# Batch 2's keys handled in the second stage, a new instruction order, paired numerators and one block-diagonal key product

## The chip, the cores and the metric

The kernel runs on one core of one Trainium2 chip. The metric is the device time of one launch in microseconds (us), on that core. Three runs of the kernel before took 995.9, 994.68 and 989.43 us; the median is 994.68 us.

## The reference

Random-feature attention, whose result is fed through a two-layer network. Cut to what matters:

```python
batch, n_heads, seq, head_dim = (8, 8, 576, 64);  n_features = 128
def phi(x):                                  # x is scaled by 64**-0.25
    h = einsum('bhsd,md->bhsm', x, omega) - sum(x * x, -1) / 2
    return exp(h - max(h, -1)) / sqrt(m)
q_p, k_p = phi(q_s), phi(k_s)
kv  = einsum('bhsm,bhsd->bhmd', k_p, v)      # one 128 x 64 matrix per batch and head
z   = sum(k_p, axis=2)
num = einsum('bhsm,bhmd->bhsd', q_p, kv)
den = einsum('bhsm,bhm->bhs', q_p, z)[..., None] + 1e-06
x   = (num / den), heads side by side        # 4608 tokens x 512
h = x @ w_in                                 # 512 -> 2048
out = (h - tanh(h)) @ w_out                  # 2048 -> 512
```

All inputs and the output are float32, and the network's weights are read as float32 too.

## The kernel before, in words

**Pairs of heads.** The eight heads are taken two at a time, so there are four pairs `c` for each batch `b`, and one unit of key work is one (batch, pair): 576 tokens of two heads, whose 64 dimensions each fill the 128 partitions.

**Chunks of tokens.** The 4608 tokens are cut into chunks by `SIZE`. For a chunk `ch` the query units (`q_unit(ch, c)`, one for each pair) give the attention result of that chunk, and the network then runs over 16 slices of 128 hidden features: 12 matmuls (L540) give `h`, ScalarE takes the tanh, VectorE subtracts, ScalarE and VectorE split the result in a high and a low part, and three matmuls for each 128 tokens (L563 to L565) add to the output. These network matmuls are of the type fp32r, with each operand split in a high and a low part, so that a product is made of three.

**Two kinds of attention work.** In the first stage, keys and queries are *native*: `native_k` and `native_q` multiply plain float32. TensorE runs each of their products as two instructions, so the trace counts two matmuls for one in the code. For one pair, `native_k` projects 4 tiles of 128 tokens for each head (L921: two products at a time, one on the upper 64 rows of the array and one on the lower), then the last 64 tokens of both heads (L923, each product 64 rows and 64 columns), takes the least of each row (L927, L936) and the exponentials (L932, L940), multiplies with the values (L944, L954), and turns the sums `z` by two transposes (L971). In the second stage, `k_unit` and `q_unit` split the operands into high and low parts and use fp32r: 9 key projections of 256 columns (L453), a rounded copy of the exponentials (`key_hi`, L715), its rest (`key_lo`, L719), the same for the values (L723, L727), and 10 products of 256 columns (L736). The sums `z` and the results are turned through DRAM there, by 12 DMAs of SyncE for each unit instead of the two of a native unit. The numerators of a query unit (L663) are plain float32 products on half the array's columns each, and VectorE multiplies them by the reciprocals (L682).

**Which batch is where.** `K2 = 4` makes the keys of batches 0, 1 and 2 native (12 units); batches 3 to 7 (20 units) are `k_unit`s. Six native query units cover the first three chunks of 256 tokens.

**The weights.** They come as 16 blocks of 1 MB in a packed form, loaded by ScalarE's queue (`d*.is`) and unpacked by ScalarE, GpSimd and VectorE (`decoder`, L1087 to L1132), while the first stage runs. A block's first network slice needs it unpacked. The network of the first 512 tokens is `feed` (`f0` to `fd`, and `f0e`, `f0f`).

**What sets the order.** The order is written out by hand, as two long strings of tokens. `ORDER` is the first stage, `LATER` the second. A token names a unit, one of its steps and places in PSUM or SBUF: `k02.pk0.2` is the first value product of batch 0, pair 2, in PSUM bank 2; `q40.m.0` is the numerators of chunk 4, pair 0. Each engine executes its own instructions strictly in this order, so an instruction that waits holds up everything behind it on its engine. `EARLY` names two loads that go to ScalarE's queue; all other loads go to SyncE's.

Of the kernel before, what the change touches and what calls it, by code (L numbers as in the profile page):

```python
# [44 lines left out]
k00.pj.2.3.4 k12.lv.2 q11.expB.1 q01.lq.0 k02.pj.5.6.7 k00.redB k00.red5 k00.expB.2 k00.redA k13.lk.0 k02.redA  # L45
k00.expA.3 k03.pj.0.1.3 k23.lk.1 k02.red5 k02.redB k03.vc k02.exp5.0 k02.expA.4 d1.is k12.vc k03.redB k02.pk0.2
k02.expB.5 k03.red5 k03.redA q01.pj.7.5 k03.exp5.1 k03.expA.6 k02.pk1 q01.redB k03.expB.7 q01.redA k13.pj.6.3.0
k02.z k13.lv.0 k02.kvf q01.expA.4 k03.pk0.1 k01.lk.2 k00.exp5.0 k13.redB q01.expB.5 k13.redA k02.zt k03.pk1
k11.lk.0 k13.expB.6 k13.red5 k23.pj.7.4.5 k02.zb k00.lv.1 k03.z k13.expA.7 q11.den0 k13.exp5.1 k03.zt d0.is
d1.b.0 k13.vc q11.nD0 k13.pk0.3 q11.nA0 k23.red5 k23.redB k03.kvf k03.zb k23.redA q11.pt0.2 d1.cl k23.expB.7  # L50
k13.pk1 q11.den1 q11.qt0.0 k11.pj.6.0.1 k13.kvf q11.nD1 k23.expA.6 q11.nA1 k13.z q01.den1 k01.lv.0 k00.vc
k23.exp5.1 q11.pt1.4 k13.kvwa k00.pk0.2 k11.red5 q11.qt1.1 k10.lk.1 q01.nA1 k11.redB q11.pn.7 k11.redA
d0.b.1 k20.lk.0 q01.nD1 k13.zt q01.den0 k00.pk1 q11.xh q10.lq.0 d0.cl k13.zb k11.expA.0 q11.xl q01.pt1.5
k23.lv.1 k00.z q01.nA0 d0.v1 k11.exp5.0 k00.zt q01.qt1.0 k01.pj.4.3.7 k01.vc k00.kvf d0.v2 k00.zb d4.is
k11.expB.1 k10.pj.6.1.5 k01.redA k01.red5 k01.expA.3 k01.redB q10.pj.2.0 k10.redA k01.expB.2 k10.redB k01.pk0.4
q01.nD0 k12.lk.2 k23.vc k10.red5 d0.v3 k23.pk0.3 k10.expA.3 k21.lk.1 k23.pk1 k10.expB.6 q10.redB q10.redA
q00.lq.0 q01.pt0.6 k01.exp5.1 k23.z d0.hi d1.v1 k01.pk1 k10.lv.1 d1.v2 d0.nh k23.zt k01.kvf k11.lv.0 d1.v3
# [1178 lines left out]
```

## Time and profile before

| | |
|---|---|
| median of 3 runs | 994.68 us (989.43 to 995.9) |
| the profiled execution | 992.21 us, its span 990.4 us |
| TensorE matmuls (PE) busy | 976.7 us, 99% |
| weight loads (PEld) | 810.1 us, 82% |
| VectorE (DVE) | 749.2 us, 76% |
| ScalarE (ACT) | 592.1 us, 60% |
| GpSimd (POOL) | 48.9 us, 5% |
| first network slice starts | 66 us |
| second chunk's network starts | 164.5 us |
| last matmul starts | 986.03 us |

The span is the part of the time that the profiler sees, so the profiled execution has 1.8 us around it. A row of the timeline gives the start of a group of equal instructions and how long it lasted to the end of its last one. Matmuls overlap, so the time that one takes from TensorE is read from the start of one row to the start of the next, not from the length of a row. A table by stage gives, for each stretch, how long each engine was busy in it and how many instructions it started.

### The profile page before, as it was taken

The page shows a single profiled execution, that of the slowest core. Times are in us where ns is not written, and L with a number is a line of the kernel's source. Part 1 is how long each engine was busy: PE and PEld are TensorE (multiplying, and loading weights), DVE is VectorE, ACT ScalarE, POOL GpSimd, SP SyncE. Part 2 cuts the span into 40 slices and gives each one's busy share as a digit, 9 for nine tenths or more (in the row PEclk, how much of TensorE's full clock was granted, in tenths as well). Part 3 has the DMA queues.
Part 4 walks back from the last instruction along what each step waited for, and adds up shares of the span by engine and source line. Part 5 has one row for each costly group of instructions (what it writes and reads, how often), then busy time and mean ns, then how long its engine had stood idle before and what let it go on. Part 6 is the DMA issues. An engine that isn't in the chain of part 4 may idle for free.

```text
span 990.4 us, 16846 instructions
## 1 busy us (share of the span) xinstructions
PE 976.7 (99%) x5260; PEld 810.1 (82%) x5260; DVE 749.2 (76%) x2772; ACT 592.1 (60%) x1497; POOL 48.9 (5%) x83
## 2 busy tenths in 40 slices
PE   9999999999999999999999999999999999999998
PEld 8787778887888888888878888788877787888886
DVE  5988887998998999989999998998577533223222
ACT  8996767685766786667656776675455332123222
...
GB/s 261 246 241 187 236 189 129 162 130 148 125 94 144 115 85 159 136 117 109 116 169 124 137 120 144 137 87 128 68 99 123 118 49 38 1 1 43 0 1 43
DMA packets 96601, 117.84 MB, mean 119 GB/s; under 512 B 19456, under 2 KB 62848, under 8 KB 96512
## 3 DMA queue, kind: packets, MB, share of 16 engines
...
q8 instruction: 42, 0.69, 0.3%
q14 instruction: 47, 0.39, 0.1%
...
## 4 chain that ended last, share of the span: by engine, by line
PE 84%; DVE 7%; ACT 3%; DMA 3%; issue 1%; SPq 1%; POOL 0%; ACTq 0%; DVEq 0%; POOLq 0%
PE h L540 35%; PE po L563 11%; PE po L565 11%; PE po L564 11%; PE pn L663 3%; PE pj_q L592 3%; PE pk L736 2%; PE k_pk L944 1%; DMA xs<-over 1%; PE pj_k_B L453 1%; PE pj_k_A L453 1%; DMA raw<-w 1%; PE k_pj L921 1%; DVE zf L1015 1%; DVE a L1118 1%
## 5 line engine op out<-in xcount | busy, mean ns | idle before, releaser
L540 PE MATMUL h<-xa,w 128*128 128x512 f32 (+2 forms) x1920 | 420.4, 368 | 1.7 <-DVE zf L551 1.7
L540 PEld LDWEIGHTS h<-xa,w 128*128 128x128 f32 x1920 | 340.5, 188 | 54.5 <-DVE zf L551 1.9
L563 PE MATMUL po<-w,zr 128*128 128x512 f32 x544 | 213.8, 393 | 0.6 <-ACT zr L553 0.6
L565 PE MATMUL po<-w,zr 128*128 128x512 f32 x544 | 212.7, 391 | 0.6 <-DVE zr L555 0.6
L564 PE MATMUL po<-w,zr 128*128 128x512 f32 x544 | 212.7, 391 | 0.0
L845 DVE TENSOR_TENSOR zf<-h,zf 128x512 f32<-128x512 f32 (+1 forms) x138 | 90.5, 656 | 147.4 <-ACT zf L844 146.0
L844 ACT ACTIVATE zf<-h 128x512 f32<-128x512 f32 (+1 forms) x138 | 78.7, 570 | 202.1 <-PE h L540 199.7
L565 PEld LDWEIGHTS po<-w,zr 128*128 128x128 f32 x544 | 102.1, 188 | 23.9 <-DVE zr L555 1.9
L563 PEld LDWEIGHTS po<-w,zr 128*128 128x128 f32 x544 | 102.2, 188 | 22.9 <-issue 3.2
L564 PEld LDWEIGHTS po<-w,zr 128*128 128x128 f32 x544 | 102.3, 188 | 16.4
L846 ACT CAST zr<-zf 128x512 fp32r<-128x512 f32 (+1 forms) x138 | 82.4, 597 | 48.8 <-DVE zf L845 47.5
L847 DVE TENSOR_TENSOR zr<-zf,zr 128x512 fp32r<-128x512 f32 (+1 forms) x138 | 90.6, 657 | 26.9 <-ACT zr L846 25.3
L611 ACT ACTIVATE phi_q<-phi_q,nb_q 128x128 f32<-128x128 f32 x240 | 80.4, 393 | 28.6 <-DVE nb_q L604 27.7
L604 DVE CUSTOM_DVE_ANT_1 phi_q<-pj_q,phi_q 128x128 f32<-128x128 f32 x240 | 57.6, 284 | 5.3 <-ACT phi_q L599 4.7
L599 ACT COPY phi_q<-pj_q 128x256 f32<-128x256 f32 x120 | 41.9, 373 | 17.2 <-PE pj_q L592 16.1
L624 DVE CUSTOM_DVE_ANT_0 zf<-phi_q,zb 128x128 f32<-128x128 f32 (+1 forms) x200 | 49.4, 287 | 2.8 <-ACT phi_q L611 2.1
L592 PE MATMUL pj_q<-om,qx 128*128 128x256 f32 x240 | 45.5, 288 | 1.2 <-DVE xs L682 0.7
L592 PEld LDWEIGHTS pj_q<-om,qx 128*128 128x128 f32 x240 | 37.6, 188 | 10.9 <-ACT zf L844 2.2
L632 DVE STREAM_TRANSPOSE phi_q<-phi_q 128x512 f32<-128x512 f32 (+1 forms) x64 | 40.3, 650 | 0.1
L470 ACT ACTIVATE phi_kA<-phi_kA,nb_k_A 128x128 f32<-128x128 f32 x80 | 27.0, 394 | 16.9 <-DVE nb_k_A L464 16.7
L470 ACT ACTIVATE phi_kB<-phi_kB,nb_k_B 128x128 f32<-128x128 f32 x80 | 27.1, 394 | 5.5 <-DVE nb_k_B L464 5.4
L663 PE MATMUL pn<-phi_q,kvw 128*64 128x64 f32 (+4 forms) x224 | 24.7, 347 | 0.0
...
## 6 DMA issues: line engine op xcount, KB each, us to landing
...
```

Of the source, the lines that this page charges most:

```text
L540: nc.tensor.matmul(o, w_, x, start=i == 0, stop=i == len(prods) - 1)
L563: nc.tensor.matmul(po[t], gh[:, 2 * j + t], wt[f][:, 0, DM:], start=first, stop=False)
L564: nc.tensor.matmul(po[t], gh[:, 2 * j + t], wt[f][:, 1, DM:], start=False, stop=False)
L565: nc.tensor.matmul(po[t], gl[:, 2 * j + t], wt[f][:, 0, DM:], start=False, stop=last)
L592: nc.tensor.matmul(u["pj", t][:, h], u["x"][:, h, t * P : (t + 1) * P], om2, start=True, stop=True)
L604: nc.vector.tensor_tensor_reduce(u["ph"][:, h, :, t], quarters(u["pj", t][:, h, :M]), u["ph"][:, h, :, t], scale=-SCALE, scalar=3.0e38, op ...
L611: nc.scalar.activation(ph, ph, AF.Exp, bias=u["nb", t][:, h : h + 1], scale=-1.0)
L663: nc.tensor.matmul(to[D * h : D * h + D, t0_:t1, a0_:a1], kvs[b, c][0][:, h], in_order(h)[:, t0_:t1, a0_:a1], start=True, stop=True)
L844: th=lambda: nc.scalar.activation(g, blocks(u["p"])[:, 0:n], AF.Tanh),
L845: g=lambda: nc.vector.tensor_sub(g, blocks(u["p"])[:, 0:n], g),
L846: gh=lambda: nc.scalar.copy(gh, g),
L847: gl=lambda: nc.vector.tensor_sub(gl, g, gh.bitcast(F32)))
```

## The change

Five edits:

- `K2` is 0, so only batches 0 and 1 have native keys (8 units), and batch 2's four units are `k_unit`s in `LATER` (24 units there).
- `SIZE`: the fifth chunk has 512 tokens instead of 384, and the last 384 instead of 512. The number of matmuls of each shape in the network stays the same.
- Both order strings are new. The numerators of two query units stand next to each other.
- The last 64 tokens of a native unit's two heads are projected by one product over all 128 rows. Its stationary operand is a block-diagonal matrix with zeros beside the two blocks, which the host lays out (`kp`, 640 columns instead of 576).
- The rounded copy `key_hi` is made by ScalarE instead of VectorE.

```diff
-SIZE = [256, 256, 256, 384, 384, 512, 512, 512, 512, 512, 512]
+SIZE = [256, 256, 256, 384, 512, 512, 512, 512, 512, 512, 384]
...
-K2 = 4
+K2 = 0
...
 ORDER = """
-q11.lq.0 k02.lv.0 k00.lk.0 k02.lk.1 q11.pj.0.1 k03.lk.2 q11.redA k03.lv.1 k02.vc q11.redB q11.expA.0
+k00.lk.0 q11.lq.0 k00.lv.0 k02.lv.1 k02.lk.1 k03.lk.2 d0.is k03.lv.2 k00.pj.0.1.2 k00.vc d1.is q11.pj.3.4 k00.redA
...
 LATER = """
-f0e.h0.6 f0e.h1 q30.ld k30.ld k30.lv f0d.o0 f0e.th f0d.o1 f0e.g q30.sa f0d.o2 q30.sv f0d.o3 f0e.gh q30.p0.0 k30.sa
+f0e.h0.6 f0e.h1 q30.ld k20.ld k20.lv f0d.o0 f0e.th f0d.o1 f0e.g q30.sa f0d.o2 q30.sv f0d.o3 f0e.gh q30.p0.0 k20.sa
...
         def key_hi(slot, g, t, m):
             u["k" + g] = ak.tile([P, 2, 2, M], F32R, tag=f"khl{slot}", name=f"khl_{n}_{g}")
-            nc.vector.tensor_copy(u["k" + g][:, :m, 0], u["ph" + g[0]][:, t : t + m])
+            nc.scalar.copy(u["k" + g][:, :m, 0], u["ph" + g[0]][:, t : t + m])
...
         def lk(slot):
-            u["f"] = ka.tile([P, S], F32, tag=f"kf{slot}", name=f"{n}_f")
-            (nc.scalar if n in EARLY else nc.sync).dma_start(u["f"], kT[c, :, b * S : (b + 1) * S])
+            u["f"] = ka.tile([P, S + D], F32, tag=f"kf{slot}", name=f"{n}_f")
+            (nc.scalar if n in EARLY else nc.sync).dma_start(u["f"], kp[b, c])
...
-            for r in rows:
-                nc.tensor.matmul(u["pj5"][r], u["f"][r, 4 * P : S], oms[r], start=True, stop=True)
+            nc.tensor.matmul(u["pj5"], u["f"][:, 4 * P :], oms, start=True, stop=True)
...
     kT = by_pair(inputs["k"])
+    kn = kT[:, :, : NN * S].reshape(NC, P, NN, S).transpose(2, 0, 1, 3)
+    kp = np.concatenate([kn, np.zeros((NN, NC, P, D), kT.dtype)], axis=3)
+    kp[:, :, D:, S:] = kp[:, :, D:, 4 * P : S]
+    kp[:, :, D:, 4 * P : S] = 0
```

Three places show what moves. In the changed program the line numbers are 13 or 14 higher: L663 is L677 there, L715 is L729, L921 is L935 and L923 is L936.

**TensorE, numerators.** Before, in the network of the second chunk: `pn_0` are the numerators of one pair, between the network's `h` matmuls and a query projection (`pj_q`), and the next pair's come 20 rows later, behind the next slice of `h`.

```order
L540 MATMUL h_2_2136<-xa,w_1186 128x256 x12
L663 MATMUL pn_0_2181<-phi_q_0_1875,k_kvw 64x384 x2
L592 MATMUL pj_q_2_0_2191<-om,qx_2_2030 128x256 x2
L736 MATMUL pk_0_2093<-khl_0_A_2131,vhl_0_A_1886 128x256 x2
L736 MATMUL pk_0_2093<-khl_0_M,vhl_0_M 128x256 x2
...
L540 MATMUL h_3_2242<-xa,w_1329 128x256 x12
L663 MATMUL pn_1_2291<-phi_q_1_2002,k_kvw 64x384 x2
L592 MATMUL pj_q_3_0_2296<-om,qx_3_2259 128x256 x2
```

With the change, at chunk 4 (`pk_3` are value products of the keys, `po` the network's output):

```order
L750 MATMUL pk_3_3050<-khl_3_B_3120,vhl_3_B_3070 128x256 x2
L677 MATMUL pn_0_3149<-phi_q_0_2261,kvw_0_2361 64x512 x2
L677 MATMUL pn_1_3157<-phi_q_1_2558,kvw_1_2826 64x512 x2
L750 MATMUL pk_3_3050<-khl_3_B_3132,vhl_3_B_3135 128x256 x2
L577 MATMUL po_2_2700<-w_1081,zr 128x512
```

The two units' numerators are now neighbours. Over the whole program the numerators of the second stage stand in 32 separate places before and in 17 now: fifteen pairs and two alone.

**TensorE, a native key projection.** Before: the end of one unit's projection and the start of the next; the two 64-column products of the last tokens are the row with x2.

```order
L921 MATMUL k_pj_152<-zf,k_f 128x128
L921 MATMUL k_pj_153<-zf,k_f 128x128
L923 MATMUL k_pj_154<-zf,k_f 64x128 x2
L921 MATMUL k_pj_174<-zf,k_f 128x128
L921 MATMUL k_pj_175<-zf,k_f 128x128
```

With the change, in the first unit, with the query projection (L1009) behind it:

```order
L935 MATMUL k_pj_137<-zf,k_f 128x128
L935 MATMUL k_pj_138<-zf,k_f 128x128
L936 MATMUL k_pj_139<-zf,k_f 128x128
L1009 MATMUL q_pj_153<-zf,q_f 128x128
L1009 MATMUL q_pj_154<-zf,q_f 128x128
```

One product of 128 partitions replaces two of 64. The first network matmul of the program is row 225 of TensorE's order before and row 178 now.

**VectorE and ScalarE, the rounded keys.** Before, on VectorE: the rounded copy (`khl`, CAST) stands between the network's subtractions and the rest that uses it (L719).

```order
L632 STREAM_TRANSPOSE phi_q_1_2002<-phi_q_1_2002 128x384
L715 CAST khl_0_A_2131<-phi_kA_0_1974 128x2x128
L847 TENSOR_TENSOR zr<-zf,zr 128x512
L719 TENSOR_TENSOR khl_0_A_2131<-phi_kA_0_1974,khl_0_A_2131 128x2x128
L744 TENSOR_TENSOR cz_0_2151<-phi_kA_0_1974 128x4x64
```

With the change, on ScalarE: it stands behind the exponentials (L484), a copy out of PSUM (L473) and the tanh (L858), ahead of the network's own rounding (L860).

```order
L858 ACTIVATE zf<-h_1_1816 128x512
L484 ACTIVATE phi_kA_0_1752<-phi_kA_0_1752,nb_k_0_A_1884 128x128 x2
L473 COPY phi_km_0_1893<-pj_k_0_M 128x128
L729 CAST khl_0_A_1895<-phi_kA_0_1752 128x2x128
L860 CAST zr<-zf 128x512
```

The copy has left VectorE's order and is one more step in ScalarE's; `key_lo` stays on VectorE and now waits for ScalarE.

More of the change, by code (lines that the diff above doesn't have):

```diff
@@ L43 @@
 ORDER = """
-q11.lq.0 k02.lv.0 k00.lk.0 k02.lk.1 q11.pj.0.1 k03.lk.2 q11.redA k03.lv.1 k02.vc q11.redB q11.expA.0
[L45 to L57, printed above, removed]
-k10.exp5.1 d0.di k23.kvwa k23.zb k12.pj.1.7.5 q01.qt0.1 q10.expB.7 k01.z k01.zt q10.expA.4 k12.redB
@@ new lines @@
+f31.th q42.sv k22.pM.7 f30.o0.2 q41.e2 q40.rw0 q40.rw1 q41.e3 f30.o1.3 q40.dr0 f31.g k22.cA0.0 q40.dr1 f30.o2.1 k22.cA1
+k22.tA0 f31.gh q40.rw2 k22.tA1 f32.h0.6 k22.eA0 q40.rw3 f31.gl q43.ld k22.eA1 f32.h1 k21.dr k22.khA0.0 k22.zA.0
+k22.khA1.1 k22.klA0 k22.cM.0 k22.klA1 q42.p0.0 f32.th k22.kvA0.4 k22.tM f31.o0 k22.zA2 q42.c0.2 f32.g k22.eM k22.vhM.0
+f31.o1 q42.t0 f32.gh k22.zM q40.rr.1 k22.khM.0 k22.vlM k22.pB0.7 q42.e0 f32.gl k22.pB1.0 k22.kvA1 k22.klM k22.cB0.0
+f31.o2 k22.cB1 k21.zr k22.vhB0.1 k21.kb k23.sa k22.kvM k22.tB0 f33.h0.6 k22.tB1 k22.vlB0 k21.zt f33.h1 k21.wv k23.sv0
@@ new lines @@
+k21.rw0 k22.eB0 k21.rw1 k22.eB1 k23.sv1 k21.rw2 q42.p1.7 q42.p2.0 f33.th k21.rw3 f32.o0 k22.zB k22.khB0.0 k30.ld
+f33.g k22.khB1.1 f32.o1 k22.vhB1.0 k22.klB0 q42.c1 k22.klB1 f33.gh f32.o2 k22.zB2 q42.c2 k22.vlB1 f33.gl k22.kvB0
+k23.lv k22.kvB1 q42.t1 f34.h0.6 k22.ca q42.t2 q42.e1 k22.cv k21.zb q42.e2 f34.h1 k22.zM2 k22.tr q42.p3.7 k22.dw0
+f34.th k23.pA0.0 k23.pA1.4 q42.c3 k22.dw1 f33.o0 f34.g k23.cA0.0 k23.cA1 q42.t3 k22.dw2 f34.gh f33.o1 k23.tA0 k22.dw3
+q42.e3 f34.gl k23.pM.7 f33.o2 k23.eA0 k23.tA1 q41.d0 k23.eA1 f35.h0.6 q41.d1 k23.khA0.0 q41.d2 k23.khA1.1 f35.h1
@@ new lines @@
+q50.rr.2 k32.zA2 k32.kvA0.4 q52.t0 k32.kvA1 q52.e0 f43.h0.6 k32.zM q52.t1 k32.khM.0 k32.vhM.0 k32.klM k32.vhB0.1
+k32.vlM q52.e1 k32.vlB0 f43.h1 k31.dr k32.pB0.0 f43.th k32.pB1.7 k32.kvM k32.cB0.0 f42.o0 f43.g k32.cB1 k32.vhB1.0
+k33.sa f42.o1 k32.tB0 k32.tB1 q52.p2.0 k32.vlB1 f42.o2 k33.sv0 k33.lv f43.gh f42.o3 k32.eB0 k33.sv1 q52.p3.7 k32.eB1
+f44.h0.6 f43.gl k40.ld k32.khB0.0 k31.zr k32.khB1.1 k31.kb q52.c2 k32.klB0 f44.h1 q52.c3 k32.klB1 k31.wv q53.sa
+k32.zB q52.t2 k32.zB2 k32.kvB0 q52.t3 k32.kvB1 f44.th k33.pA0.0 k31.zt k33.pA1.7 k32.ca k32.zM2 k31.rw0 f43.o0
@@ new lines @@
+k40.tM q52.rw0 q60.sv k40.eM f48.o3 k40.cB0.0 q52.rw1 k40.cB1 q52.rw2 k41.sa k40.kvA0.4 q52.rw3 k40.kvA1 f49.gl
+f4a.h0.6 k33.rw0 k40.tB0 k33.rw1 k40.khM.0 k40.tB1 k33.rw2 k40.eB0 k40.klM k33.rw3 f4a.h1 k40.eB1 k40.zM q52.dr0
+k41.sv0 k40.khB0.1 q52.dr1 k40.vhM.0 q61.ld k40.klB0 k40.vhB0.1 q60.p0.0 f4a.th k40.zB q60.p1.7 f49.o0 k40.vlM
+q52.rr.0 q60.c0.0 k40.zB2 q60.c1 f4a.g f49.o1 k40.vlB0 f4a.gh q60.t0 k40.kvM k40.kvB0 q60.t1 q60.e0 k33.zb q60.p2.0
+f49.o2 f4a.gl k40.khB1.0 k40.vhB1.0 q60.d0 f49.o3 q60.e1 k40.klB1 q60.c2 k40.vlB1 q60.p3.7 f4b.h0.6 k40.zM2 k41.lv
@@ L366, with favor_attention_ffn @@
+fae.o2 faf.gl faf.o0 faf.o1 sa.c0.1 faf.o2 sa.d0 sa.c1.2 sa.c2.0 sa.ce sa.d1 sa.d2 sa.de
 """
 @with_exitstack
-def favor_attention_ffn(ctx: ExitStack, tc: tile.TileContext, qT, kT, va, vt, omT, w, out):
+def favor_attention_ffn(ctx: ExitStack, tc: tile.TileContext, qT, kT, kp, va, vt, omT, w, out):
     nc = tc.nc
@@ L1224 @@
         "kT": kT,
+        "kp": np.ascontiguousarray(kp),
         "va": np.ascontiguousarray(va),
```

613 lines of the change are left out of this document (310 added, 303 removed).

## The prediction

> **What bounds the kernel now.** I read the page's busy times first, then a table by stage, then TensorE's timeline. The page:
>
> ```profile
> span 990.4 us, 16846 instructions
> PE 976.7 (99%) x5260; PEld 810.1 (82%) x5260; DVE 749.2 (76%) x2772; ACT 592.1 (60%) x1497; POOL 48.9 (5%) x83
> PE 84%; DVE 7%; ACT 3%; DMA 3%; issue 1%; SPq 1%; POOL 0%; ACTq 0%; DVEq 0%; POOLq 0%
> ```
>
> TensorE is busy for 99% of the span and holds 84% of the chain that ended last. Only 13.7 us are idle, so nothing large can be won from waits; what TensorE no longer has to issue is what counts. Whether it becomes time depends on the other engines, stage by stage (the columns are the stretch and its length, and then each engine's busy time with its instructions; the last are granted clock, DMA share and GB/s):
>
> ```profile
> 0.00:66.00 66.00, 61.57 (x610) 52.33 (x611) 52.05 (x162) 58.99 (x187) 17.57 (x44) 1.00 0.82 250
> 66.00:115.50 49.50, 46.98 (x236) 37.79 (x235) 39.06 (x71) 36.02 (x55) 18.78 (x19) 1.00 0.84 217
> 115.50:164.50 49.00, 48.61 (x240) 39.10 (x241) 38.48 (x83) 34.12 (x61) 12.56 (x20) 1.00 0.70 177
> 164.50:305.60 141.10, 140.65 (x832) 121.46 (x832) 130.73 (x586) 100.29 (x276) 0.00 (x0) 1.00 0.49 133
> 305.60:494.10 188.50, 187.79 (x1005) 159.68 (x1005) 176.24 (x740) 131.23 (x360) 0.00 (x0) 1.00 0.45 121
> 494.10:708.00 213.90, 213.32 (x1095) 174.70 (x1094) 193.62 (x808) 139.78 (x378) 0.00 (x0) 1.00 0.46 122
> 820.00:990.40 170.40, 166.42 (x733) 136.61 (x731) 48.44 (x71) 41.45 (x69) 0.00 (x0) 1.00 0.04 15
> ```
>
> The first stretch ends where the network's first slice starts: ScalarE is busy for 89% of it and DMA for 82%, beside TensorE's 93%. From 164.5 to 708 us VectorE is busy for 500.6 of 543.5 us, 92%, and TensorE idles for only 1.7 us. From 820 us TensorE works alone. The granted clock is 1.00 throughout, so no term comes from the clock.
>
> **The change part by part: batch 2's keys.** What a native unit takes from TensorE is read from start to start:
>
> ```profile
> 14.88 1.16 PE L921 MATMUL k_pj<-zf,k_f 64*128 64x128 f32 x16
> 15.97 0.44 PE L923 MATMUL k_pj<-zf,k_f 64*64 64x128 f32 x4
> 16.34 1.11 PE L944 MATMUL k_pk<-k_v,zf 128*128 128x66 f32 x8
> 17.28 0.38 PE L971 MATMUL k_pk<-zf,k_z 128*128 128x128 f32 x2
> 17.50 1.00 PE L944 MATMUL k_pk<-k_v,zf 128*128 128x66 f32 x8
> 18.34 0.44 PE L954 MATMUL k_pk<-k_v,k_ph 128*128 128x132 f32 x2
> 18.72 1.16 PE L921 MATMUL k_pj<-zf,k_f 64*128 64x128 f32 x16
> ```
>
> From 14.88 to 18.72 stand one projection, one first and one second value product and one turning of the sums: 3.84 us, one whole unit. What a unit of the second stage takes stands in this stretch, which serves the numerators below too:
>
> ```profile
> 453.08 0.39 PE L564 MATMUL po<-w,zr 128*128 128x512 f32 x1
> 453.31 0.39 PE L565 MATMUL po<-w,zr 128*128 128x512 f32 x1
> 453.62 1.08 PE L663 MATMUL pn<-phi_q,kvw 128*64 128x256 f32 x8
> 454.64 0.50 PE L736 MATMUL pk<-khl_M,vhl_M 128*128 128x256 f32 x2
> 454.98 0.39 PE L736 MATMUL pk<-khl_B,vhl_B 128*128 128x256 f32 x2
> 455.21 0.40 PE L453 MATMUL pj_k_B<-om,kx 128*128 128x256 f32 x2
> ```
>
> Two fp32r products of 256 columns take 0.23 us (454.98 to 455.21), so the 19 of a unit take 2.2 us. Four units move: 4 x (3.84 - 2.2) = 6.6 us less. The lower bound: two such products take 0.34 us behind the numerators (454.64 to 454.98); if every pair cost that, a unit would take 3.2 us and the four would save 2.5. I take 6.6, since most products stand among other fp32r matmuls.
>
> **The block-diagonal product.** It replaces four instructions that take 0.37 us (15.97 to 16.34) by two over the whole array, in each of 8 remaining units. The trace has no such product beside the warm-up:
>
> ```profile
> 1.06 3.61 PE L419 MATMUL warm<-zf 128*128 128x128 f32 x16 [1.06 <-DVE zf L416]
> ```
>
> By the transposes of the same size (L971, two in 0.22 us) a unit saves 0.15 us, 1.2 in all; by the warm-up (0.226 us each, 0.45 for two) it loses 0.08, 0.6 in all. I take 0.5 us saved, nearer to the transposes, which are in the same stage. It carries 32 KB of zeros more for a unit. [...]
>
> **Numerators in pairs.** Entering and leaving them costs something. The matmul ahead takes 0.31 us instead of 0.23 (453.31 to 453.62, against 453.08 to 453.31), and the pair behind 0.34 instead of 0.23: together 0.19. Inside there is a fixed part, found from a smaller visit:
>
> ```profile
> 222.69 0.87 PE L663 MATMUL pn<-phi_q,k_kvw 128*64 128x384 f32 x4
> 223.48 0.50 PE L563 MATMUL po<-w,zr 128*128 128x512 f32 x1
> ```
>
> 384 tokens take 0.79 us, 512 take 1.02 (453.62 to 454.64). So 128 tokens cost 0.23, 384 should cost 0.69, and 0.10 is fixed. A visit thus costs 0.29 us beside its columns. There are 32 visits before and 17 after: 15 x 0.29 = 4.4 us less; 2.9 if the inner part stays. A pair adds a wait: if the second unit's turned exponentials are late, TensorE stands between the two, and the network's matmuls queued behind wait with it; VectorE's two multiplications then follow each other, and hold both banks longer.
>
> **Casts and the other engines.** VectorE loses its 100 rounded copies, and ScalarE gets 120:
>
> ```profile
> L715 DVE CAST khl_B<-phi_kB 128x256 fp32r<-128x256 f32 x40 | 11.5, 288 | 1.7 <-ACT phi_kB L470 1.6
> L715 DVE CAST khl_A<-phi_kA 128x256 fp32r<-128x256 f32 x40 | 11.0, 284 | 1.1 <-ACT phi_kA L470 1.1
> L715 DVE CAST khl_M<-phi_km 128x128 fp32r<-128x128 f32 x20 | 4.3, 217 | 0.2 <-PE pk L736 0.2
> L459 ACT COPY phi_kA<-pj_k_A 128x256 f32<-128x256 f32 x40 | 13.6, 376 | 3.4 <-PE pj_k_A L453 3.3
> L464 DVE CUSTOM_DVE_ANT_0 phi_kA<-pj_k_A,phi_kA 128x128 f32<-128x128 f32 x80 | 19.3, 283 | 0.0
> L719 DVE TENSOR_TENSOR khl_A<-phi_kA,khl_A 128x256 fp32r<-128x256 f32 x40 | 16.5, 418 | 0.1
> L444 DVE TENSOR_TENSOR kx<-kf,kx 64x576 fp32r<-64x576 f32 x20 | 15.1, 754 | 0.5
> ```
>
> That takes 26.8 us from VectorE and puts about 40 on ScalarE (0.34 us each, 13.6/40). Four more units put about 12 us each on VectorE: two splittings (0.75 each), nine projections (0.28 and a short read), five rests of 0.42 or less, and some twenty smaller ones near 0.28 (an estimate from these rows). The second stage's VectorE work goes from 500.6 to about 522 us while its TensorE time grows by 4 x 2.2 and shrinks by 4.4: from 92% to 95% busy. ScalarE gets about 8 us with each unit (the same steps' copies and exponentials, an estimate), and goes from 371 to about 445 of 548 us, 81%. Both stay below TensorE, so the edit costs nothing as long as the steps stand early enough in the new order. Without that cover one miss costs what this row shows:
>
> ```profile
> 513.37 0.50 PE L453 MATMUL pj_k_A<-om,kx 128*128 128x256 f32 x2 [0.48 <-DVE xs L682]
> ```
>
> In the first stage four units leave with their ScalarE and DMA work (2.5 MB), but the 16 MB of weights must come in a shorter time, so DMA stays near its 0.82; the weights' loads are issued earlier in the new order. SyncE gets 40 more DMAs, ten for each moved unit, in stretches where DMA is busy for less than half. The new chunk sizes change no count of matmuls, and the end stays one copy and one store. For tighter engines I add 2.5 us of new waits (bounds: 4 less, since the first 66 us hold 4.4 idle that a shorter stage could shed; 8 more).
>
> **Sum.** -6.6 - 0.5 - 4.4 + 2.5 = -9.0. The profiled span of 990.4 becomes 981.4, and with the 1.8 us around it (992.21 - 990.4) 983.2. The three runs (989.43, 994.68, 995.9) lie on both sides of the profiled one, their median 2.5 above it; I forecast 984.0.
>
> **The rivals.**
> - *The waits shrink too.* The first stage gets lighter for ScalarE, which is its tightest engine after TensorE, and 4 us of its idle time go; with the terms at their upper ends (6.6, 1.2, 4.4) this gives 992.2 - 16.2 = 976. For it: ScalarE's 89% in the first stretch. Against: the ratio of ScalarE to TensorE there hardly changes, both lose about a quarter. Chance 0.15.
> - *VectorE becomes the bound of the second stage.* At 95% each late step of a query unit delays a numerator pair or a projection; 25 misses of 0.48 us take all of 11.5 us back: about 993. For it: the 92% already there. Against: TensorE idles for 1.7 us at that load. The chance, with all other ways to come out near zero, is 0.15.
> - *Slower: the rounded keys are late on ScalarE.* Each copy now queues in order behind exponentials and a tanh, `key_lo` waits for it, and TensorE's value product for that. The sum turns to a loss when the 120 copies cost TensorE 0.10 us each on average (11.5/120), and to a loss of 1% above 0.18. At 0.2 us each, 24 us, the time is 992.2 - 11.5 + 24 = 1005. For it: the strict order. Against: ScalarE has a fifth of its time free, and the products can stand further back. Chance 0.10.
> - *The pairs do not merge* (the second is late and the first's exit is paid anyway): 4.4 us are not won, 988. This lies in the forecast's range.
>
> **How the numbers follow.** The forecast's own range is 979 to 989, chance 0.60; the others have 0.15, 0.15 and 0.10. Two runs of this kernel can differ by 0.65%, so about 1% can be told from no change; 1% below the median is 984.7. A little over half of the forecast's case lies below that (0.33), and the first rival (0.15): 0.48 faster. The rest of the forecast (0.27) and VectorE's case (0.15) are within 1%: 0.42. Slower: 0.10. The range from 975 to 997 leaves out most of the slower case and a tail of the fastest.
>
> **What would show it.** Right: TensorE's instructions fall by 100, from 5260 to 5160; the first network slice starts near 50 us instead of 66 (66 - 4 x 3.84); 17 visits of numerators, each pair of 512-token units lasting some 1.94 us instead of 2 x 1.02; the block-diagonal row near 0.25 us; TensorE still 99% busy; VectorE near 763 us and ScalarE near 650 in all, since four native units leave with some 7 and 15 us (estimates). Wrong: TensorE idle for over 20 us, with VectorE or ScalarE as the releaser; long rows of waiting at the value products L750; or the first slice later than 54 us.

## The result and the profile after

The changed kernel took 1001.89 us (median of 6 runs, 998.9 to 1005.39), the kernel before 993.54 us on the same chip (6 runs, 989.43 to 995.9). The ratio is 1.0079, its 95% interval 1.0054 to 1.0105: slower by 0.8%, and above the predicted range. The profiled execution took 1005.39 us, the longest of the six, so that the losses read from it are larger than the median's; its span is 1003.6. The page of the changed kernel:

```profile
span 1003.6 us, 16903 instructions
PE 983.1 (98%) x5160; PEld 821.4 (82%) x5160; DVE 760.0 (76%) x2821; ACT 637.5 (64%) x1664; POOL 47.4 (5%) x79
PEclk8799999999999999999999999999999999999999
```

TensorE has the 5160 instructions that were forecast, VectorE and ScalarE are busy for 760.0 and 637.5 us (forecast 763 and 650). But TensorE's busy time rose from 976.7 to 983.1 with 100 instructions fewer, and the row of the granted clock, all nines before, starts with 8 and 7. The table by stage shows where (the last three columns are granted clock, DMA share and GB/s; chunk 2's network starts at 170.6 us, where it started at 164.5 before):

```profile
0.00:16.20 16.20, 13.81 (x116) 12.33 (x116) 7.41 (x17) 9.54 (x30) 2.58 (x13) 1.00 0.87 315
16.20:29.90 13.70, 13.70 (x82) 12.17 (x81) 5.78 (x10) 7.67 (x24) 1.93 (x3) 0.50 0.84 252
29.90:43.50 13.60, 11.74 (x71) 9.58 (x71) 12.83 (x65) 10.61 (x33) 7.25 (x14) 0.62 0.36 110
43.50:62.20 18.70, 17.35 (x161) 13.52 (x159) 15.45 (x52) 17.44 (x49) 3.69 (x9) 1.00 0.42 119
62.20:120.30 58.10, 53.12 (x265) 43.13 (x266) 49.94 (x109) 42.49 (x76) 20.59 (x25) 0.94 0.88 237
120.30:170.60 50.30, 48.18 (x222) 39.10 (x221) 32.38 (x50) 31.41 (x51) 11.35 (x16) 0.97 0.59 151
170.60:1003.60 833.00, 825.18 (x4253) 691.60 (x4251) 636.24 (x2524) 518.35 (x1408) 0.00 (x0) 1.00 0.38 105
```

Up to 170.6 us TensorE idles for 12.7 us (170.6 less the six busy times), against 7.3 before in the stretch up to 164.5. The rest of the loss does not look like idling: from 16.2 to 29.9 us TensorE is busy throughout, at half its clock, and issues 82 instructions where the stretch ahead of it, with 2.4 us idle, had 116. The missing share of the clock times the length gives an estimate of the work lost in the stretches from 16.2 us on: 6.8 us at a clock of 0.50, then 5.2 at 0.62, 3.5 at 0.94 and 1.5 at 0.97, 17 in all. Behind 170.6 the clock is 1.00. DMA is busy for 0.87 and 0.84 in the first 30 us, then for 0.36 and 0.42, then for 0.88 (before: 0.82 up to 66 us). It looks as if some loads come too early and others too late.

How it begins stands in two timelines. ScalarE, then TensorE:

```profile
13.05 1.12 ACT L1100 ACTIVATE a<-raw 128x1024 f32<-128x1024 f32 x1 [1.19 <-DMA raw<-w]
14.07 0.26 ACT L980 COPY kvf<-k_pk 128x128 f32<-128x128 f32 x1
```

```profile
12.81 0.49 PE L936 MATMUL k_pj<-zf,k_f 128*128 128x128 f32 x2
14.38 0.43 PE L984 MATMUL k_pk<-zf,k_z 128*128 128x128 f32 x2 [1.08 <-DMA k_f<-kp]
14.70 3.06 PE L957 MATMUL k_pk<-k_v,k_phi 128*128 128x66 f32 x16
```

ScalarE's first step on weight block 0 (`d0.b`, L1100) waits 1.19 us for its load. The copy of k00's sums (L980) stands behind it, and k00's transposes (L984), which use the same PSUM tile, start right after that copy. The row names a load of keys as the releaser; in e1_filler below, the same transposes are released by that copy (`ACT kvf`). At 16.2 us the clock halves: the 16 products of L957 last 3.06 us.

This gap is not there in every execution. e3_loads below has the same order up to 24 us, and in its profile the block's load came in time and nothing waits ahead of the transposes:

```profile
13.01 0.49 PE L936 MATMUL k_pj<-zf,k_f 128*128 128x128 f32 x2
13.34 0.39 PE L984 MATMUL k_pk<-zf,k_z 128*128 128x128 f32 x2
```

Its clock halves at 16.9 us, in a wait of 1.13 us for a query's load. So the rows at 13 us show one way into the half clock, not the only one.

### The profile page after: what moved, and what is told of

It is laid out like the page before. It is cut to its first block, busy times and chain, and to the rows that moved or that the text cites. A ratio compares the mean times of both kernels' runs of the same rounds, so it can differ in the third digit from the quotient of the medians.

```text
span 1003.6 us, 16903 instructions
## 1 busy us (share of the span) xinstructions
PE 983.1 (98%) x5160; PEld 821.4 (82%) x5160; DVE 760.0 (76%) x2821; ACT 637.5 (64%) x1664; POOL 47.4 (5%) x79
## 4 chain that ended last, share of the span: by engine, by line
PE 76%; DVE 10%; DMA 6%; ACT 4%; issue 3%; SPq 1%; POOL 0%; ACTq 0%; DVEq 0%; POOLq 0%
PE h L554 32%; PE po L577 10%; PE po L578 10%; PE po L579 10%; PE pk L750 3%; PE pj_q L606 2%; PE pn L677 2%; DMA w<-a 2%; PE k_pk L957 1%; PE pj_k_B L467 1%; DMA cz<-turned_k 1%; PE pj_k_A L467 1%; DMA raw<-w 1%; DMA zb<-zd 1%; DVE zf L859 1%
## 5 line engine op out<-in xcount | busy, mean ns | idle before, releaser
L554 PE MATMUL h<-xa,w 128*128 128x512 f32 (+2 forms) x1920 | 426.0, 371 | 5.0 <-DMA w<-a 4.8
L579 PE MATMUL po<-w,zr 128*128 128x512 f32 x544 | 213.1, 392 | 2.3 <-DVE zr L569 2.3
L858 ACT ACTIVATE zf<-h 128x512 f32<-128x512 f32 (+1 forms) x138 | 78.7, 571 | 186.6 <-PE h L554 185.3
L579 PEld LDWEIGHTS po<-w,zr 128*128 128x128 f32 x544 | 102.1, 188 | 25.1 <-DVE zr L569 2.9
L860 ACT CAST zr<-zf 128x512 fp32r<-128x512 f32 (+1 forms) x138 | 82.4, 597 | 47.4 <-DVE zf L859 46.7
L638 DVE CUSTOM_DVE_ANT_0 zf<-phi_q,zb 128x128 f32<-128x128 f32 (+1 forms) x240 | 57.4, 285 | 4.0 <-DMA zb<-zd 1.6
L484 ACT ACTIVATE phi_kA<-phi_kA,nb_k_A 128x128 f32<-128x128 f32 x96 | 32.2, 395 | 9.3 <-DVE nb_k_A L478 9.0
L484 ACT ACTIVATE phi_kB<-phi_kB,nb_k_B 128x128 f32<-128x128 f32 x96 | 31.6, 396 | 1.6 <-DVE nb_k_B L478 1.6
L677 PE MATMUL pn<-phi_q,kvw 128*64 128x64 f32 (+4 forms) x272 | 26.8, 342 | 0.0
```

The costliest lines, as they stand in the source:

```text
L484: nc.scalar.activation(u[kind][:, at + i], u[kind][:, at + i], AF.Exp, bias=w["nb"][:, i : i + 1], scale=-1.0)
L554: nc.tensor.matmul(o, w_, x, start=i == 0, stop=i == len(prods) - 1)
L579: nc.tensor.matmul(po[t], gl[:, 2 * j + t], wt[f][:, 0, DM:], start=False, stop=last)
L638: nc.vector.tensor_tensor_reduce(quarters(junks[h][r]), u["ph"][r, h, :, t], quarters(kvs[b, c][1][r, h]), scale=1.0, scalar=EPS, op0=ALU. ...
L858: th=lambda: nc.scalar.activation(g, blocks(u["p"])[:, 0:n], AF.Tanh),
L860: gh=lambda: nc.scalar.copy(gh, g),
```

## The experiments

Theory A: the gap at 13 us halves the clock, and the half clock is the loss. Theory B: the stage's own products lower the clock, whatever the gap. Theory C: weights issued too late are the loss. Each row below has the median, its ratio to the kernel before in the same comparison, and from the trace the starts of the first network slice and of chunk 2's network (before: 66.0 and 164.5). The starts are those of one profiled execution each: that of the changed kernel is the slowest of its runs, those of e4_both and e16_noload are the fastest of theirs, so starts and medians do not always go together. Runs of one group were measured beside each other: e1 to e4, e5 to e8, e9 to e11, e12 to e15, e16 and e17. Between groups, a difference by the medians and one by the ratios can be 2 us apart.

| run | us | ratio (95%) | first slice | chunk 2 |
|---|---|---|---|---|
| changed kernel | 1001.89 | 1.0079 (1.0054 to 1.0105) | 62.2 | 170.6 |
| e1_filler | 1002.49 | 1.0080 (1.0048 to 1.0113) | 58.0 | 166.7 |
| e2_d0b | 1002.08 | 1.0077 (1.0051 to 1.0103) | 59.7 | 165.7 |
| e3_loads | 997.97 | 1.0034 (1.0017 to 1.0051) | 60.7 | 165.3 |
| e4_both | 997.52 | 1.0034 (1.0013 to 1.0055) | 57.2 | 161.8 |
| e5_spread | 999.38 | 1.0021 (0.9990 to 1.0052) | 59.1 | 163.6 |
| e6_oldorder | 999.07 | 1.0016 (0.9986 to 1.0047) | 63.4 | 163.9 |
| e7_two64 | 1002.28 | 1.0048 (1.0021 to 1.0075) | 57.9 | 166.3 |
| e8_before_early | 1003.08 | 1.0055 (1.0022 to 1.0087) | 71.7 | 171.2 |
| e9_fill | 993.89 | 0.9978 (0.9950 to 1.0006) | 56.8 | 158.8 |
| e10_lo | 1019.49 | 1.0235 (1.0193 to 1.0276) | 58.2 | 186.2 |
| e11_lo4 | 1019.04 | 1.0236 (1.0189 to 1.0283) | 58.0 | 185.6 |
| e12_nov | 997.96 | 1.0016 (0.9985 to 1.0048) | 59.2 | 164.9 |
| e13_nodec | 991.81 | 0.9957 (0.9927 to 0.9988) | 56.5 | 154.2 |
| e14_order | 996.59 | 1.0030 (1.0006 to 1.0054) | 58.8 | 161.9 |
| e15_orderfill | 994.08 | 0.9986 (0.9960 to 1.0013) | 57.0 | 159.1 |
| e16_noload | 995.40 | 1.0012 (0.9985 to 1.0038) | 55.1 | 158.8 |
| e17_casts | 999.19 | 1.0054 (1.0027 to 1.0082) | 76.0 | 174.3 |
| e18_vec | 1006.74 | 1.0100 (1.0051 to 1.0149) | 59.6 | 161.7 |

**e1_filler**

```diff
         def zt():
+            if n == "k00":
+                filler = ps.tile([P, P], F32, tag="po1", name="filler")
+                for _ in range(5):
+                    nc.tensor.matmul(filler, ident, ident, start=True, stop=True)
```

> Ten more matmul instructions (five products of the identity with itself into a free PSUM bank, their result unused) stand ahead of the first unit's transposes (k00.zt), where TensorE idled 1.08 us at 13.3 us in the changed kernel. Theory A (that gap is what halves the granted clock; the clock then stays at 0.5 from 16.2 to 29.9 us and, behind a second gap that the slow stage makes, from 33.3 to 43.5): clock 1.00 up to 33 us at least, the first network slice near 51 to 55 us instead of 62.2, time 1001.9 - 7 to - 12, so 990 to 995. Theory B (the stage's own products, half an array high or 66 columns wide, lower the clock whatever the gap): clock 0.5 from 16.2 as before, time 1002. Theory C (the weights' loads come too late and set the pace): the first slice comes earlier, but TensorE waits longer for the decoded weights at 84 to 130 us; time no better than 998.

**e2_d0b**

```diff
 k00.pk1 k02.redB k10.lk.1
-d0.b.0
 k02.redA
...
-d0.cl
...
 k02.expB.5
+d0.b.0 d0.cl
 k02.pk0.3
...
 k02.z
+d0.v1 d0.v2
 k02.kvf
...
-d0.v1
...
-d0.v2
```

> Only the order string differs: ScalarE's first step on weight block 0 (d0.b, which waited 1.19 us for its load at 13.05 us in the changed kernel and held up the copy of k00's sums) stands behind k02's exponentials, with the steps that need it moved back as far. Theory A (ScalarE's wait for the load makes TensorE's gap, and the gap halves the clock): no gap over 0.6 us and clock 1.00 up to 43 us, first slice near 50 to 53 us, 990 to 995. Theory B (the products themselves lower the clock): half clock at 16 us all the same, 1002. Theory C (late loads set the pace): first slice earlier, longer waits for decoded weights at 84 to 130 us, no better than 998.

In both profiles the gap is closed and the clock does not halve at 16.2 us; the time stayed. In e1_filler the half clock came later (columns as above):

```profile
0.00:29.00 29.00, 24.02 (x224) 21.13 (x224) 16.19 (x45) 20.44 (x64) 5.85 (x19) 1.00 0.92 309
29.00:39.20 10.20, 9.88 (x51) 8.10 (x52) 9.50 (x46) 7.18 (x23) 5.36 (x12) 0.50 0.31 100
```

With TensorE earlier, other waits came up: 1.28 us for a query's load at 22.8 us, 1.53 at the transposes at 27.8. In e2_d0b 1.26 us came up at 17.3 behind ScalarE and 1.92 at 22.5 for a query's load, and the clock was 0.50 from 24.2 to 41.3. So A as the whole cause falls, and B too as far as it has the clock halve without a gap. That gaps lower the clock fits both runs, but since the gap at 13 us can be absent without any edit, they do not show it; e9_fill does.

**e3_loads and e4_both**

```diff
 k03.zb
+d3.is
...
 q11.qt0.0
+d4.is
...
 q11.qt1.1
+d5.is
...
 k10.kvwa k10.kvf
-d3.is
+d6.is
...
-d4.is
+d7.is
...
```

> Only the places of the weight loads' issues in the order string differ: blocks 3, 4 and 5 are issued in the stretch from 24 to 45 us, where DMA is busy for 0 to 0.4, and each later block at the place of the one three before it. Theory C: TensorE's waits for decoded weights (excess of 2.9, 2.4 and 2.3 us at 84, 108 and 129 us) and the half-clock window of 3.4 us behind each vanish, 7.6 + 3 x 1.7 = 12.7 us less, 989 to 992, with the first 44 us as in the changed kernel (first slice near 62). Theory A alone (the first 44 us are the whole loss): 1000 to 1003.

> The edits of the two runs before together. Theories A and C together: the gains add, 1001.9 - 10 - 12 = 978 to 984, clock 1.00 throughout, which is what the prediction's sum gave (983). A alone: as the second run, 990 to 995. C alone: as the third, 989 to 992. If the stage that starts earlier runs into the same loads sooner, the gains overlap: 985 to 988.

Issuing the loads earlier is worth 3.9 us (1001.89 to 997.97), a third of what C expected; of the waits at 84, 108 and 129 us the first two stayed (3.84 and 2.00 us), the third is gone. The move of e2_d0b adds nothing to it. In e4_both the first network slices still wait, though block 3 was issued at 25.9 us instead of 47.2:

```profile
78.87 0.71 PE L555 MATMUL h<-xa,w 128*128 128x512 f32 x2
83.39 1.22 PE L555 MATMUL h<-xa,w 128*128 128x512 f32 x2 [3.82 <-DMA w<-a]
```

It is the last step of the block's chain, the DMA that adds its low half; one of these took 11.0 us to land.

**e5_spread** (e4_both, with the loads of blocks 1 and 2 some 10 us later, blocks 3 to 8 one after the other behind them, and the rest earlier)

> The order of the run e4_both with the weight loads spread over the stage: block 1's is issued some 12 us later, block 2's some 8 us later, blocks 3 to 8 one after the other up to about 54 us. Where it comes from: in the run before, DMA moved 371 to 402 GB/s with a share of 1.00 to 1.04 from 5 to 20 us, TensorE waited 1.06 and 1.82 us for query loads at 16.6 and 23.9 us, and DMA's share fell to 0.15 at 50 to 55. Theory D (two weight blocks ahead of the keys fill DMA, and the late key and query loads make the gaps that halve the clock): both waits for q_f vanish or fall below 0.6 us, the clock stays 1.00 up to 45 us, first network slice at 50 to 53 us instead of 57.2, and 988 to 992 us. Rival (the query load is late because SyncE's own queue holds it behind loads that wait for their places): waits for q_f and half clock as before, 996 to 998.

No gain: the wait for the query's load at 24 us shrank to 0.40 us, as D had it, but 1.57 came up at 16.5 us behind ScalarE, and the clock halved at 19.6.

**e6_oldorder** (the order string of the kernel before without its tokens `k20` to `k23`)

> The changed kernel, but the first stage in the order of the kernel before, with batch 2's tokens left out of it; everything else as changed (block-diagonal product, rounded copies on ScalarE, second stage). Theory E (the new order of the first stage is what loses, not the move of batch 2): the first stage's excess of 33 us falls to near the 10 us of before, clock 1.00, and the time is 980 to 986. Rival F (with four units of TensorE work gone the stage is set by the weights' chain, whatever the order): the stage's waits for decoded weights grow to 10 us or more, 990 to 998.

Neither theory as it stands. The old order is the better one: against e7_two64, which is the changed kernel but for one product and was measured beside it, it takes 3.2 us less (999.07 against 1002.28), and is level with the kernel before (its interval holds 1). But its first stage ends at 163.9 us where the kernel before, with 15.4 us more of TensorE work in it, took 164.5; the waits are now for VectorE and ScalarE (2.98 us for L565 at 111, 2.02 for L1064 at 61, and 1.29, 1.34 and 1.42 at 36, 51 and 59), not for weights. So the new order, its early loads included, explains about 3 us; that the forecast's gain is missing shows in either order.

**e7_two64**

```diff
-            nc.tensor.matmul(u["pj5"], u["f"][:, 4 * P :], oms, start=True, stop=True)
+            for h, r in enumerate(rows):
+                nc.tensor.matmul(u["pj5"][r], u["f"][r, 4 * P + D * h : 4 * P + D * h + D], oms[r], start=True, stop=True)
```

> The changed kernel with the block-diagonal product taken back: two products of 64 rows and 64 columns from the same tile, as before; the loads stay as they are. By the rows of the traces the two ways take 0.33 and 0.37 us a unit, so 8 units give 0.3 us: no difference that can be measured, 1001 to 1003. If the whole-array product is what starts the trouble (it takes longer or feeds the clock gate differently), the clock at 16 us stays 1.00 and the time falls to 990 to 997.

As expected: no difference that can be measured (1002.28 against 1001.89 us, and the intervals of the two ratios overlap).

**e8_before_early**

```diff
 k03.lk.2
+d0.is d1.is
 q11.redA
```

> The kernel before with one edit: the loads of weight blocks 0 and 1 are issued right behind the first key loads (at about 3 us, as the changed kernel does at 5.0 and 6.5) instead of 19.2 and 10.4. Theory D: DMA is full in the first 15 us, the keys and queries come up to 5 us later (2 MB at 400 GB/s), TensorE gets a gap of over 1 us and half-clock windows, first network slice at 69 to 74 us instead of 66, 998 to 1003. Rival (these loads have room): no change, 993 to 995.

(The two loads leave their later places.) Theory D, shown on the kernel before: two loads that come earlier cost 8.6 us by the medians, 0.2 to 0.9% by the interval. Its timeline on TensorE, and the stretch behind it:

```profile
11.94 1.57 PE L942 MATMUL k_pk<-k_v,k_phi 128*128 128x66 f32 x8 [1.10 <-POOL k_v L910]
15.90 2.08 PE L994 MATMUL q_pj<-zf,q_f 64*128 64x128 f32 x16 [2.40 <-DMA q_f<-qT]
```

```profile
12.50:22.70 10.20, 7.80 (x51) 6.91 (x50) 1.61 (x4) 5.50 (x23) 0.20 (x1) 0.50 0.50 173
```

The clock halves at 12.5 us, behind the wait of 1.10, and is 0.50 for 10.2 us; in them a query's load comes 2.40 us late. The first slice moves from 66.0 to 71.7.

**e9_fill** (e4_both with 41 unused products)

```diff
+    def fill(o, k):
+        for _ in range(k):
+            nc.tensor.matmul(o, ident, ident, start=True, stop=True)
...
             u["pj"] = [ps.tile([P, 4, M], F32, tag=BANKS[i], name=f"{n}_pj{h}") for h, i in enumerate(slots)]
+            fill(u["pj"][0][:, 0], {"q01": 4, "q00": 7}.get(n, 0))
...
```

> The run e4_both with unused products (identity times identity) in six of TensorE's longest gaps of that run's trace: 4 and 7 ahead of the query projections that waited 1.06 and 1.82 us at 16.6 and 23.9 us, 6 and 2 ahead of the transposes that waited 1.53 and 0.75 at 29.2 and 31.9, 14 and 8 inside the network's slices that waited 3.82 and 2.16 at 83.4 and 106.9 (0.22 us each, so they fit into the gaps). Nothing that TensorE waits for is changed. Theory A' (each gap costs itself and, behind it, 3.4 to 10 us at half clock, so that the clock's part is about 7 us of the profiled run and 9 of the median, whose granted clock is 0.991): clock 0.997 to 1.00, 987 to 991 us. Theory F' (the stage is set by the other engines and by DMA, and TensorE at half clock only fills time in which it would wait): the clock is 1.00, the waits grow by as much, 995 to 999.

Between the two theories: 993.89 us.

```profile
span 991.6 us, 17060 instructions
PE 975.5 (98%) x5242; PEld 817.3 (82%) x5242; DVE 759.9 (77%) x2821; ACT 636.7 (64%) x1664; POOL 48.0 (5%) x79
PEclk9999999999999999999999999999999999999999
```

The clock is 1.00 up to the last matmuls with 82 instructions more (in the 12 runs 0.996 to 1.00, in those of e4_both 0.986 to 0.993): with these gaps filled the clock stayed up. The time is 3.6 us less than e4_both (997.52) by the medians and 5.6 by the ratios, not the 9 that its clock of 0.991 stood for. A part of the clock's loss was cover: at half clock TensorE filled time in which it would have waited. Ahead of chunk 2's network it idled for 14.9 us in e4_both; here the fillers take 10.4 and 8.0 us of idling are left, 3.5 more together. This run is level with the kernel before (its interval holds 1).

**e10_lo and e11_lo4**

```diff
-            nc.scalar.activation(wt[f][:, 1], u["af"], AF.Copy, scale=-1.0)
+            pass
...
-            nc.gpsimd.dma_start(wt[f][:, 1], u["af"], accum_op=ALU.add)
+            nc.gpsimd.tensor_sub(wt[f][:, 1], u["af"], wt[f][:, 0].bitcast(F32))
```

> The changed kernel with the low halves of the weights made in another way: GpSimd subtracts the rounded half from the decoded block, instead of ScalarE writing the negative (1.07 us each, 16 of them) and a DMA adding the block to it (5.1 to 11 us from issue to landing). Same result, same order string. This takes 17 us from ScalarE, 8 MB of accumulation from DMA and some 5 us from each block's chain. Theory C' (the weights' chain makes the waits from 75 to 135 us): the waits L554 <- DMA w<-a (4.8 us in all) vanish with the half-clock windows at 88, 112 and 132 us; 992 to 996. Theory F' (ScalarE, with 45 us of work ahead of the first slice, also sets the first 60 us): three blocks are decoded there, 3 us less in front too; 988 to 993. Theory A alone (the first 44 us are all): 999 to 1003.

> The run e4_both (997.5 us) with the low halves made by GpSimd as in the run e10_lo. Theories C' and F' together: the 3.99 us of waiting at 79 us and the half clock behind it (6.8 us, 3.4 lost) go, the first slice comes 1 to 3 us earlier, 986 to 990 us. If GpSimd's subtraction slows VectorE beside it, or the wait moves to VectorE's decoding steps: 994 to 998.

A miss: 17.6 and 21.5 us slower than their bases. Rows of e10_lo's groups:

```profile
L1145 POOL TENSOR_TENSOR w<-a,w 128x1024 fp32r<-128x1024 f32 x16 | 42.2, 2638 | 25.2 <-ACT w L1139 25.2
L1123 DVE SCALAR_TENSOR_TENSOR a<-raw,a 128x1024 uint32<-128x1024 uint32 x16 | 29.4, 1836 | 0.2
```

GpSimd's subtraction takes 2.64 us, and VectorE's step L1123 takes 1.84 us on the mean, up to 3.47, where it took 1.31 at most in the changed kernel. TensorE's waits for VectorE's `zr` (L579) rose to 14.3 us. So these two say nothing on C.

**e12_nov and e13_nodec**

```diff
+        step1 = step2 = step3 = lambda: None
```

```diff
+        clamp = step1 = step2 = step3 = minus_hi = lambda: None
...
-            nc.gpsimd.dma_start(wt[f][:, 1], u["af"], accum_op=ALU.add)
+            nc.gpsimd.dma_start(wt[f][:, 1], u["af"])
```

> The run e4_both without VectorE's three decoding steps of each weight block (the output is then not the reference's: the weights stay undecoded). They are 0.68, 1.22 and 1.22 to 1.48 us each, so 9.4 us leave VectorE's 41.3 ahead of the first slice and 44 its 82 behind it; everything else stays. Theory V (VectorE's work, in its strict order, is what now sets the stage): first slice at 50 to 53 us instead of 57.2, no wait at 79 to 86 us, second chunk's network at 150 us instead of 161.8, time near 985. Theory S (ScalarE and late loads set it): less than 3 us in all, 995 to 998.

> As e12_nov, and without GpSimd's clamp and ScalarE's negative half as well (1.2 and 1.07 us a block; the DMA then copies instead of adding, in the same number and size). Another 3.2 us less of ScalarE's 45.2 ahead of the first slice, 14 behind it. Theory V: as e12_nov within 2 us. Theory S: 3 to 6 us less than e12_nov, most of it ahead of the first slice. If neither e12_nov nor this shortens the stage (first slice later than 55 us in both), neither engine's load but the loads' arrival and the order's own chain set it.

The base e4_both, e12_nov and e13_nodec, each ahead of the first slice and from there to chunk 2's network:

```profile
0.00:57.20 57.20, 48.31 (x424) 40.88 (x425) 41.33 (x141) 45.18 (x134) 16.53 (x39) 0.94 0.80 270
57.20:161.80 104.60, 98.63 (x485) 80.24 (x486) 82.10 (x158) 73.51 (x125) 31.74 (x41) 0.97 0.69 174
```

```profile
0.00:59.20 59.20, 51.67 (x424) 43.61 (x424) 32.81 (x132) 45.15 (x134) 14.73 (x38) 0.86 0.77 260
59.20:164.90 105.70, 99.03 (x484) 80.68 (x485) 41.60 (x118) 72.96 (x125) 30.05 (x41) 0.97 0.68 172
```

```profile
0.00:56.50 56.50, 49.41 (x424) 41.32 (x424) 32.03 (x132) 42.55 (x131) 11.42 (x36) 0.91 0.80 282
56.50:154.20 97.70, 95.94 (x485) 79.00 (x485) 39.51 (x119) 60.69 (x111) 10.96 (x27) 1.00 0.54 181
```

VectorE's time falls by half behind the first slice (82.10 to 41.60), and this stretch gets no shorter at the same clock: VectorE's decoding is not its bound. Without ScalarE's and GpSimd's steps and the adding the stretch falls by 6.9 us, some 3 of them by the clock (0.97 to 1.00), and the median from 997.96 to 991.81. The chain of a weight block through ScalarE, GpSimd and the adding DMA costs that; which of the three, no run here shows. Ahead of the first slice the two settle less: a query's load came 2.66 and 2.87 us late there and the clock was lower than in the base.

**e14_order and e15_orderfill** (e4_both with `q00.lq.0` moved behind `q01.lq.0`, the loads of blocks 7 to 9 issued earlier, and those of 10 to 15 later; then the fillers of e9_fill in smaller numbers)

> The run e4_both with two more moves in the order string: the query load that TensorE waited for at 23.9 us (1.82 us; q00) is issued ahead of three key loads that wait for their places, and the weight blocks 10 to 15 are issued behind the stretch from 65 to 85 us, in which DMA moved 240 to 315 GB/s and one block's accumulation took 11.0 us to land instead of 5.8. Theory D (late loads make the gaps): no wait for q_f over 0.6 us, the wait of 3.8 us for the weights at 83 us falls below 1, clock 0.995 or more, 986 to 990 us. Rival (the other engines' order): waits move to VectorE and ScalarE, 995 to 998.

> The run e14_order with unused products in the places of e9_fill, fewer where the loads should now come in time (2 and 2 ahead of the query projections, 6 and 2 at the transposes, 6 and 8 in the network). If the clock was the rest: 1.00, and 2 to 4 us less than e14_order. If e14_order already runs at full clock: the fillers cost up to 3 us where no gap is left.

The rival's side for e14_order: the wait at 83 us is gone, but the queries' loads still come 0.99 and 1.14 us late, 2.33 us came up at the transposes behind GpSimd and 1.73 at 123 us for weights, and the wait behind VectorE at 101 us stayed (2.44). The fillers are worth 2.5 us here (4.4 by the ratios).

**e16_noload**

```diff
+            if f < 3:
+                u["raw"] = blank
+                return
             u["raw"] = places[f].tile([P, 2 * DM], U64, tag=f"w{f}", name=f"raw{f}")
...
+    blank = places[13].tile([P, 2 * DM], U64, tag="w13", name="blank")
+    nc.gpsimd.memset(blank.bitcast(F32), 0.0)
```

> The run e4_both without the loads of weight blocks 0 to 2 (a tile of zeros stands for them, so the output is not the reference's); their decoding, all other loads and the order stay. It takes 3 MB from the first 25 us, in which DMA moved 371 to 402 GB/s at a share of 0.9 to 1.04: 7.7 us of it. Theory D (late loads make the gaps of the first 50 us): no wait for q_f over 0.3 us, clock 1.00 up to 45 us, first slice at 50 to 52 us instead of 57.2, 989 to 991. Theory K (the chain of small steps through the engines, each in its strict order): the waits at the transposes and at 46 to 53 us stay, first slice at 55 to 57, 995 to 998.

Theory K's side: the waits for queries are gone and the first slice comes at 55.1 us, 2.1 earlier, not 6; 1.57 us at the transposes behind ScalarE's copy, 1.33 behind VectorE and 0.80 at 51 us are there. With these loads away TensorE still idles for 6.9 us ahead of the slice and stands at half clock for 6.8 us (28.5 to 35.3). By the releasers in the rows, what it waits for there is the order's own chain of small steps through four engines.

**e17_casts and e18_vec**

```diff
-            nc.vector.tensor_copy(u["k" + g][:, :m, 0], u["ph" + g[0]][:, t : t + m])
+            nc.scalar.copy(u["k" + g][:, :m, 0], u["ph" + g[0]][:, t : t + m])
```

(e18_vec is the reverse of this, in e9_fill.)

> The kernel before with one edit of the change: the 100 rounded copies of the keys on ScalarE instead of VectorE, in the same places of the order. The forecast's step (ScalarE has room for them): VectorE loses 26.8 us, ScalarE gets about 34, TensorE's waits change by less than 2 us, 992 to 996. The rival of the prediction (each copy behind ScalarE's queue costs TensorE 0.2 us): 20 us more, 1012 to 1016.

> The run e9_fill (clock 1.00, 993.9 us) with the 120 rounded copies of the keys back on VectorE; the first stage is untouched. If copies on ScalarE cost TensorE in the new order what they cost in the old one (4.2 us behind 164.5 us in the profile of e17_casts, 0.04 us each), this is 4 to 5 us faster: 989 to 990. If the new order is laid out for them, VectorE's load goes from 760 to some 790 us (0.27 us each), and the second stage gets slower: 995 to 1003, with waits of TensorE for VectorE.

In e17_casts chunk 2's network starts 9.8 us late, at half clock from 12.4 to 36.3 us, where no copy was moved; behind that, to the last matmul, it takes 825.7 us where the kernel before took 821.5. So 100 copies cost 4.2 us in the old order, and not by the clock: the four runs of e17_casts with a mean clock of 0.999 or more took 995.14 to 998.79 us, the 18 such runs of the kernel before 989.86 to 994.94. In the new order the copies are better on ScalarE: with them on VectorE this stretch takes 839.3 us instead of 827.9, though nothing ahead of it was changed. The second stage of e9_fill, then of e18_vec (the two stretches end at different instructions):

```profile
158.80:705.00 546.20, 542.81 (x2906) 456.26 (x2905) 511.48 (x2157) 422.36 (x1203) 0.00 (x0) 1.00 0.49 133
161.70:715.00 553.30, 546.86 (x2882) 452.64 (x2881) 526.65 (x2256) 388.96 (x1079) 0.00 (x0) 1.00 0.49 131
```

VectorE goes from 93.6% to 95.2% busy, and TensorE loses 11 us over the stage. Its idle time grows only from 3.7 to 6.4 us, so most of the loss stands in its busy time; that VectorE's load makes it is argued.

## Why the prediction was wrong

**TensorE's own work was right.** A pair of numerators of 512 tokens takes 1.92 us (forecast 1.94), in 17 places:

```profile
544.44 1.99 PE L677 MATMUL pn<-phi_q,kvw 128*64 128x128 f32 x32
546.36 0.74 PE L750 MATMUL pk<-khl_B,vhl_B 128*128 128x256 f32 x4
```

From chunk 2's network to the last matmul the forecast had 4 x 2.2 more for batch 2 and 4.4 less for the pairs: 821.5 + 4.4 = 825.9 us. Measured: 828.2 (826.2 to 830.3 in the runs that keep this second stage). No run takes the pairs, the chunk sizes and the second stage's order apart. The reading that TensorE works alone from 820 us is not right, since VectorE and ScalarE are busy for 48.44 and 41.45 of 170.40 us there; nothing in the sum rests on it.

**The block-diagonal product** was to save 0.5 us. Ahead of a value product it takes 0.33 us from TensorE:

```profile
10.18 0.49 PE L936 MATMUL k_pj<-zf,k_f 128*128 128x128 f32 x2
10.51 1.00 PE L957 MATMUL k_pk<-k_v,k_phi 128*128 128x66 f32 x8
```

Ahead of a projection or of numerators it takes 0.42 (at 6.5, 47.6 and 60.1 us). The two small products took 0.36 or 0.37 in either place, so there is nothing saved that can be measured, as e7_two64 has it; the term was 0.5 us too large.

**The step that failed** is the first stage's share: the sum books the 3.84 us of each native unit, 15.4 in all, as time. Three sentences of the prediction let it. "The granted clock is 1.00 throughout, so no term comes from the clock": true of the trace before, not of a stage with longer gaps. "DMA stays near its 0.82; the weights' loads are issued earlier": DMA's share up to the first slice fell to 0.62; two blocks were issued ahead of most keys (by 5.0 and 6.5 us, instead of 10.4 and 19.2), the fifth and sixth later than before (63.1 and 70.7, instead of 55.7 and 60.8). And "I add 2.5 us of new waits". Batch 2 and the small products were to bring chunk 2's network from 164.5 to 148.6 us; it starts at 170.6. The 22.0 us between are 5.4 of more idling (12.7 against 7.3) and 17 of half clock, in the profiled execution. The first slice was forecast for 50 us; it starts at 62.2, and no run came below 55.1. Two of the prediction's own signs of being wrong are there: that slice, and TensorE idle for 20.5 us of the span (its longest waits, 4.8 us in all, are for the weights' DMA, not for VectorE or ScalarE).

What the runs put in its place: with four native units gone from it, the first stage does not get shorter by their 15.4 us, in the old order (e6_oldorder) or the new. TensorE now waits for late steps of the other engines and for loads, and behind such gaps stood 3.4 us (the changed kernel at 87.9) to 23.9 us (e17_casts at 12.4) at half clock. That the four units had hidden these steps is argued from the waits; no run puts other work in their place and takes out the rest. By the medians, the new order makes 3 us of the loss (e6_oldorder against e7_two64), the places of the later loads 4 (e3_loads, e4_both), the clock's own part 2.5 to 3.6 (e15_orderfill, e9_fill; 4.4 and 5.6 by the ratios), the weights' chain behind ScalarE and GpSimd up to 6 (e13_nodec). They overlap, and all of them together were not tried. What holds the first 55 us once the first loads are out of it is argued from e16_noload's waits, not settled.

**The casts** were put at nothing. They cost 4.2 us in the old order; no run separates what they cost in the new one, where VectorE is worse for them. The slower rival named 1005 us, near the time measured, by a mechanism that is not the cause: 0.04 us a copy instead of 0.2, and the loss stands ahead of 170 us, where there is no copy. VectorE as the bound was near: with 20.8 us more on VectorE, e18_vec loses 11 us.

No version here that gives the right result is clearly faster than the kernel before; e9_fill and e15_orderfill are level with it.
